# A list scheduler with other durations and a table of places, and block means spread by POOL

## The chip, the core and the metric

The kernel runs on one core of a Trainium2 chip. A core has TensorE (PE, with its weight loads listed as PEld), VectorE (DVE), ScalarE (ACT), GpSimd (POOL) and the queue of SyncE (SP), from which this kernel issues its DMAs. Each engine works through its own instructions in the order in which they were written and waits for the others by semaphores. The metric is the device time of one execution in microseconds, given as the median of several runs.

## What is computed

Four batches of 768 tokens with eight heads of 64. Each query sees its neighbours closer than 16 positions and, besides, 24 block keys and values, the maximum of 32 keys and the mean of 32 values. The attended rows pass through a mixer: one product pair over the tokens, with a residual, and one over the channels, with a residual. All is fp32.

```python
k_sum = k.reshape(B, H, nb, block, D).max(axis=3)
v_sum = v.reshape(B, H, nb, block, D).mean(axis=3)
...
a = np.exp(scores_all)
a = a / (np.sum(a, axis=-1, keepdims=True) + 1e-09)
v_all = np.concatenate([v, v_sum], axis=2)
return np.matmul(a, v_all).astype(np.float32)
...
h = np.maximum(xt @ w_tok1, 0.0) @ w_tok2
u = x + h.transpose(0, 2, 1)
h2 = np.maximum(u @ w_ch1, 0.0) @ w_ch2
return (u + h2).astype(np.float32)
```

## The kernel before

**What a batch does.** Heads are worked in pairs `p`, four to a batch. For each pair `scores` forms two groups `g` of score tiles in PSUM (L467). DVE masks each tile and takes its lowest value (`lowest`, L481), ACT takes the exponential and its sum (`power`, L491), twelve of each for a pair. In batches 0 and 1 `turn` transposes the result on PE (L529) and ACT evicts it (L540); in the later batches DVE and DMAs do so. `weighted` multiplies with the values (L599), POOL and DVE make the reciprocals (L605, L625), DVE scales (L610). `tok1` (L753) and `tok2` (L912, L920) are the two token products, `ch1` (L981) and `ch2` (L1024) the channel products, one slot for each of 24 blocks of the hidden layer. Each value is kept as a high and a low half, so a product is three matmuls. The last batch uses a scheme with fewer multiplications on sums of blocks of the weights; `mixes` makes these weight sums on POOL and ACT during the earlier batches and writes them to DRAM.

**The start.** There is no other batch to work on while the attention of batch 0 runs, which uses the PSUM banks `att`, `acc0` and `acc1`. Meanwhile the weights arrive as 64-bit words and are converted: `w_tick` `i` issues two DMAs (L1635), then an absolute value on ACT (L1665), a clamp on POOL (L1669), three integer operations on DVE (L1674, L1681, L1688), and, apart from the first three ticks, high halves on ACT (L1712) and low halves on POOL (L1718). Ticks 0 to 2 are the weight of `tok1`, 3 to 5 that of `tok2`, the rest the channel weights in the order in which `ch1` and `ch2` use them.

**Block keys and block means.** `key_blocks` takes the maxima of a pair's keys on DVE (L335) and copies them beside each window (L344). In batch 0 `first_means` makes the block means of a pair's values: 48 small matmuls (L361) leave two partial sums for each of the two heads in PSUM; ACT copies one of each to SBUF (L372). For the first head DVE adds the other (L382, `once`) and POOL spreads the result over the twelve tiles of the values (L387, `spread`). For the second head one DVE instruction adds and spreads at once (L375, `both`).

**What sets the order.** Nothing is issued directly. Every step is a `Work` handed to `Plan.add` with an engine, a duration ("hold") in microseconds, what it reads and writes, and a rank. `Plan._order` then plays the kernel: an engine that is free takes, of the works that are ready by the played clock, the one of least rank and, within a rank, of least number `seq`. The ranks are `R_H` 0, `R_EVAC` 1, `R_ATT` 2, `R_LATER` 3, `R_W` 4 and `R_MIX` 6. A work is ready when all that it needs has ended in the play, with an allowance `LATE` after another engine's work; a DMA takes its kilobytes by `RATE`, plus `LAND`. The order found so is written out and is the order of each engine's queue on the chip. The holds therefore do not change any instruction, but they decide which one stands ahead of which. `behind` holds a work back until another one has begun.

Of the kernel before, what the change touches and what calls it, by code (L numbers as in the profile page):

```python
# [15 lines left out]
ALU = mybir.AluOpType  # L16
# [55 lines left out]
class Work:  # L72
    def __init__(self, seq, eng, took, run, rank, kb):
        self.seq, self.eng, self.took, self.run, self.rank, self.kb = seq, eng, took, run, rank, kb
        self.takes, self.needs, self.behind = [], set(), set()
        self.start = self.end = None


class Plan:
    LATE = {"pe": 0.3, "act": 0.15, "dve": 0.15, "pool": 0.2, "sp": 0.0}  # L80
    RATE, LAND = 250.0, 2.2
# [46 lines left out]
    def _order(self):  # L128
# [9 lines left out]
        idle = {e: 0.0 for e in self.LATE}  # L138
        queues = {e: [] for e in self.LATE}
# [5 lines left out]
        for w in self.works:  # L145
            if not left[w]:
                release(w)
        while events:
# [51 lines left out]
def tile_attention_mixer(  # L200
# [89 lines left out]
    def load(slot, view, src, kb, reads=(), behind=()):  # L290
        return add(
            "sp", 0.06, lambda: nc.sync.dma_start(out=view(slot.t), in_=src),
# [13 lines left out]
    def load_v(n):  # L306
# [7 lines left out]
        state["v"] = load(slot, lambda t: t[:WIN], vw[b, h], 295)  # L314
        if b > 0:
            s = vs[b]
            add(
                "sp", 0.06,
# [9 lines left out]
    def key_blocks(p):  # L328

        if p >= B * NP:  # L330
# [3 lines left out]
            "dve", 0.98,  # L334
# [8 lines left out]
            "dve", 0.33,  # L343
# [7 lines left out]
    def first_means(p):  # L351
# [22 lines left out]
        def both(n):  # L374
            nc.vector.tensor_tensor(  # L375
                out=v_t[n].t[WIN:NC],
                in0=half(1, 1).unsqueeze(1).broadcast_to([NB, NT, D]),
                in1=s.t[WIN:NC, D:].unsqueeze(1).broadcast_to([NB, NT, D]), op=ALU.add,
            )

        def once():
            nc.vector.tensor_tensor(  # L382
                out=s.t[WIN:NC, :D], in0=half(0, 1), in1=s.t[WIN:NC, :D], op=ALU.add
            )

        def spread(n):
            nc.gpsimd.tensor_copy(  # L387
                v_t[n].t[WIN:NC], s.t[WIN:NC, :D].unsqueeze(1).broadcast_to([NB, NT, D])
# [3 lines left out]
            "pe", 0.9, sums, reads=[(v_t[2 * p], 0), (v_t[2 * p + 1], 0)], writes=[(pt, 0)],  # L392
# [1504 lines left out]
```

## Time and profile before

| | us |
|---|---|
| median of 3 runs | 560.07 |
| lowest and highest of them | 559.93, 560.61 |
| the profiled execution | 559.61 |
| its span, first to last instruction | 557.8 |

The profiled execution spends 1.81 us outside of its span. The rows that the prediction shows are of three kinds. Window rows give the busy time of each engine in a stretch, with the number of instructions. Timeline rows give start, duration, engine, line, operation, what it writes and reads, a count, and in brackets the idle time of the engine just before, with what ended it. Group rows give the sum and the mean of all instructions of one line and form.

### The profile page before, as it was taken

What the parts mean: (1) busy time and instruction counts of PE and PEld (TensorE: products, weight loads), DVE (VectorE), ACT (ScalarE), POOL (GpSimd) and SP (SyncE); (2) the same over time, 40 slices, a digit from 0 to 9 for tenths busy, and PEclk for the clock granted to TensorE, in tenths of its full rate; (3) what the DMA queues carried; (4) which work ended last, traced back from release to release, by engine and by line L of the source; (5) the groups of instructions that cost most, each with busy time, mean ns of one, the idle gap of its engine ahead of it and who ended that gap; (6) DMA issues with size and microseconds to landing.
All of it is one profiled execution on the core that took longest, in us unless ns stands there. A gap on an engine that the chain in (4) does not pass through costs nothing.

```text
span 557.8 us, 12595 instructions
## 1 busy us (share of the span) xinstructions
PE 544.0 (98%) x4557; PEld 479.6 (86%) x4557; DVE 330.3 (59%) x922; ACT 251.9 (45%) x784; POOL 246.8 (44%) x362
## 2 busy tenths in 40 slices
PE   7699999999999999999999999999999999999997
PEld 4588788888999978888799988878889999999997
DVE  4788999979365355454543247454352065669992
ACT  4786666625585344332323325343433453356410
POOL 0326687835574932310067404378769963000000
PEclk9999999999999999999999999999999999999999
DMA  8963668755668138768595316787696543932742
GB/s 277 330 189 108 215 209 249 240 163 190 203 187 251 42 131 226 198 207 226 146 253 137 104 29 196 160 237 198 171 259 168 135 155 116 333 95 81 219 134 85
DMA packets 125743, 101.10 MB, mean 181 GB/s; under 512 B 70000, under 2 KB 105456, under 8 KB 125680
## 3 DMA queue, kind: packets, MB, share of 16 engines
q1 hardware_dynamic: 125680, 100.29, 60.7%
q8 instruction: 36, 0.59, 0.5%
q14 instruction: 27, 0.22, 0.1%
HBM read 70.18 MB, written 28.31 MB: 177 GB/s over the span
## 4 chain that ended last, share of the span: by engine, by line
PE 90%; ACT 4%; DVE 3%; POOL 2%; issue 1%; ACTq 0%
PE acc L1024 27%; PE hp L981 27%; PE sc L467 4%; PE av L599 4%; PE up L920 3%; PE t1q L837 3%; ACT e L491 2%; PE x L1251 2%; PE y L1251 2%; PE z L1251 2%; PE pz L1251 2%; PE t1q L800 2%; PE up L1213 2%; PE warm L1731 1%; PE pw L1251 1%; PE pv L1251 1%
## 5 line engine op out<-in xcount | busy, mean ns | idle before, releaser
L1024 PE MATMUL acc<-h,w2h 128*128 128x256 f32 (+1 forms) x576 | 153.8, 339 | 0.0
L981 PE MATMUL hp<-u,w1h 128*128 128x256 f32 (+1 forms) x576 | 143.8, 339 | 0.0
L1024 PEld LDWEIGHTS acc<-h,w2h 128*128 128x128 f32 x576 | 100.6, 188 | 13.8 <-ACT h L993 1.6
L981 PEld LDWEIGHTS hp<-u,w1h 128*128 128x128 f32 x576 | 98.0, 189 | 12.4 <-issue 1.1
L981 PE MATMUL hp<-u,w1l 128*128 128x256 f32 (+1 forms) x288 | 96.9, 336 | 0.0
L491 ACT ACTIVATE e<-e,den 128x120 f32<-128x120 f32 x192 | 73.3, 384 | 52.0 <-DVE den L481 39.1
L1024 PE MATMUL acc<-h,w2l 128*128 128x256 f32 (+1 forms) x288 | 96.4, 335 | 0.0
L998 DVE SCALAR_TENSOR_TENSOR h<-hp,h 128x512 fp32r<-128x512 f32 (+1 forms) x72 | 39.9, 554 | 90.9 <-ACT h L993 90.7
L993 ACT ACTIVATE h<-hp 128x512 fp32r<-128x512 f32 (+1 forms) x72 | 35.2, 489 | 114.7 <-PE hp L981 114.5
L981 PEld LDWEIGHTS hp<-u,w1l 128*128 128x128 f32 x288 | 54.4, 189 | 5.8
L1024 PEld LDWEIGHTS acc<-h,w2l 128*128 128x128 f32 x288 | 54.2, 188 | 5.2
L481 DVE CUSTOM_DVE_ANT_0 e<-sc,mask_sb 128x120 f32<-128x120 f32 x192 | 41.7, 277 | 16.8 <-PE sc L467 16.2
L605 POOL TENSOR_SCALAR rec<-den 128x6 f32<-128x6 f32 x32 | 8.6, 269 | 66.1 <-ACT e L491 64.0
L491 ACT ACTIVATION_READ_ACCUMULATOR e<-e,den 128x1 f32 x192 | 36.1, 188 | 0.0
L1064 POOL TENSOR_TENSOR ot<-ot,u 128x512 f32<-128x512 f32 (+1 forms) x24 | 24.4, 1042 | 19.7 <-DVE ot L1056 18.2
L467 PE MATMUL sc<-k,q 64*64 64x120 f32 x768 | 28.0, 271 | 3.7 <-DVE den L481 2.2
L467 PEld LDWEIGHTS sc<-k,q 64*64 64x64 f32 x768 | 20.5, 132 | 12.5 <-issue 6.2
L920 PE MATMUL up<-wt2h,t 128*128 128x512 f32 (+1 forms) x96 | 28.4, 354 | 0.6 <-DVE t L739 0.6
L599 PEld LDWEIGHTS av<-v,eT 120*64 120x64 f32 x768 | 24.0, 138 | 4.7 <-issue 2.8
L599 PE MATMUL av<-v,eT 120*64 120x64 f32 x768 | 26.5, 224 | 0.9 <-PE hp L981 0.4
L335 DVE TENSOR_REDUCE ks<-k 128x24 f32<-128x768 f32 x16 | 15.2, 948 | 20.5 <-DMA k<-in_kw 20.5
L423 DVE TENSOR_REDUCE vs<-vb 96x8 f32<-96x256 f32 (+1 forms) x40 | 17.8, 458 | 9.4 <-DMA vb<-in_vb 9.3
(248 smaller groups left out, 1042.7 us busy)
## 6 DMA issues: line engine op xcount, KB each, us to landing
w<-in_w_ch SPq DMA_DIRECT2D x48, 256.0 KB
k<-in_kw SPq DMA_DIRECT2D x16, 720.0 KB
v<-in_vw SPq DMA_DIRECT2D x32, 288.0 KB
q<-in_q SPq DMA_DIRECT2D x16, 384.0 KB
away<-e SPq DMA_DIRECT2D x16, 384.0 KB
eT<-away SPq DMA_DIRECT2D x64, 96.0 KB
w<-in_w_tok SPq DMA_DIRECT2D x12, 256.0 KB
vb<-in_vb SPq DMA_DIRECT2D x32, 96.0 KB
```

Source lines behind the costliest of these rows:

```text
L423: lambda: nc.vector.tensor_reduce(out=s.t[:VB, rows], in_=slot.t[:VB], axis=AX, op=ALU.add),
L467: nc.tensor.matmul(tiles[j].t[c * QT : (c + 1) * QT, i * NC : (i + 1) * NC], lhsT=qt.t[rows, t * QT : (t + 1) * QT], rhs=kt.t[rows, t, :], ...
L481: nc.vector.tensor_tensor_reduce(out=e.t[:, j, i * P : i * P + NC], in0=tiles[j].t[:, i * NC : (i + 1) * NC], in1=mask_sb[:, mv, :], op0=A ...
L491: nc.scalar.activation(ei, ei, AF.Exp, bias=den_t[n].t[:, 1, T : T + 1], scale=-1.0, accum_out=den_t[n].t[:, 0, T : T + 1],)
L599: nc.tensor.matmul(pv[cs, T], lhsT=eT[:NC, T % (TT // 2), cs], rhs=v.t[:NC, 2 * T + c], start=True, stop=True,)
L920: nc.tensor.matmul(pt.t[:, :nt], lhsT=t1.t[:, part, ks], rhs=w.t[:, k, h0 : h0 + nt], start=(far and k == 0 and i == 0), stop=(k == DTOK / ...
L981: nc.tensor.matmul(pt.t[:, :nt], lhsT=block(w, f, c), rhs=us[c].t[:, part], start=(i == 0), stop=(i == len(ops) - 1),)
L993: lambda: nc.scalar.activation(h.t[:, 0], pt.t[:, :nt], AF.Relu),
L998: lambda: nc.vector.scalar_tensor_tensor(out=h.t[:, 1], in0=pt.t[:, :nt], scalar=0.0, in1=h.t[:, 0].bitcast(F32), op0=ALU.max, op1=ALU.sub ...
L1024: nc.tensor.matmul(slot.t[:, c0 : c0 + nt], lhsT=block(w, f, o), rhs=h.t[:, part], start=(f == 0 and w == "w2h" and part == 0 and o % n == 0),
L1064: lambda view=view, u=u: nc.gpsimd.tensor_tensor(out=view(), in0=view(), in1=u.t[:, 1].bitcast(F32), op=ALU.add),
L1251: nc.tensor.matmul(pt.t[:, :cols], lhsT=w[wp][0](), rhs=z.t[:, zp], start=first and seen == 0, stop=final and seen == 3 * len(ops) - 1, sk ...
```

## The change

It has five parts.

1. The play in `Plan` gets other constants: first times for each engine (`FIRST`), a time after the hold in which the result becomes visible (`DRAIN`), a time in which the waiting engine notices (`NOTICE`), and a DMA that takes `BEGIN`, kilobytes by 375, and `LAND`.
2. Nearly every hold is replaced. A DMA issue on SP is 0.44 instead of 0.06, and the kilobytes of value loads and of weight loads are given as 413 and 375 instead of 295 and 262.
3. `Work.place` takes the part of (rank, seq) in the play's queues, and the table `PLACES` gives 45 works of the start, by number, another place.
4. In `first_means` the second head is treated as the first: `once` on DVE, `spread` on POOL; `both` is gone.
5. `TOKT` goes from 3 to 7, so ticks 3 to 6 get rank 2 instead of 4; and the weight sum `('w2', 4, 'h')` is handed in at slot 21 of batch 2 instead of slot 14, held behind the `ch1` of that slot.

The numbers in `PLACES` count the works of the changed kernel. Read in the code, they are: the second pair's first value load ahead of the first pair's second (9); the queries of pair 3 (128); thirteen of `lowest`, ten of pairs 1 and 3 to the front (108, 114, 116, 118, 237 to 247) and three of pairs 0 and 2 to behind later works (20, 22, 140); exponentials (23, 56, 60, 145, 273); evictions (51, 182, 184, 316); `once` and `spread` (123, 125, 217, 219, 284, 286) and a partial sum (216); scalings, reciprocals and low halves on DVE (97, 188, 192, 197, 255); steps of ticks 2 to 6 (88, 153, 163, 173, 227); the copy of block keys (147); on PE one `tok1` (261), one transpose (289), and the second score group of pair 3, which goes from rank 0 to rank 4 (267).

```diff
+        self.place = (rank, seq)
...
+PLACES = {
+    9: (0, 7.1), 20: (2, 61.7), 22: (2, 63.4), 23: (1, 128.8), 51: (1, 128.9), 56: (1, 128.2),
+    60: (1, 128.7), 88: (2, 14.2), 97: (2, 190.5), 108: (2, 13.9), 114: (2, 16.1),
+    116: (2, 62.6), 118: (2, 16.3), 123: (2, 16.2), 125: (2, 63.2), 128: (0, 7.7),
+    140: (2, 206.8), 145: (4, 305.5), 147: (2, 206.1), 153: (2, 206.2), 163: (2, 206.4),
+    173: (2, 78.1), 182: (2, 247.5), 184: (2, 247), 188: (2, 190.7), 192: (2, 15.6),
+    197: (2, 278.5), 216: (4, 392.4), 217: (2, 205.4), 219: (2, 14.8), 227: (4, 505.6),
+    237: (2, 15.5), 239: (2, 13.8), 241: (2, 15.3), 243: (2, 190), 245: (2, 14.3),
+    247: (2, 14.8), 255: (2, 204.8), 261: (2, 197.9), 267: (4, 618.7), 273: (4, 506.5),
+    284: (2, 79.8), 286: (2, 79.2), 289: (2, 198.6), 316: (4, 391.6),
+}
...
-    LATE = {"pe": 0.3, "act": 0.15, "dve": 0.15, "pool": 0.2, "sp": 0.0}
-    RATE, LAND = 250.0, 2.2
+    FIRST = {"pe": 1.17, "act": 1.9, "dve": 0.85, "pool": 1.2, "sp": 0.7}
+    DRAIN = {"pe": 0.16, "act": 0.1, "dve": 0.08, "pool": 0.045, "sp": 0.0}
+    NOTICE = {"pe": 0.035, "act": 0.035, "dve": 0.035, "pool": 0.09, "sp": 0.035}
+    SEEN, BEGIN, LAND, RATE = 0.06, 1.34, 1.0, 375.0
...
+        w.place = PLACES.get(w.seq, w.place)
...
-                    heapq.heappush(queues[w.eng], (w.rank, w.seq, w))
+                    heapq.heappush(queues[w.eng], (w.place, w.seq, w))
...
-                    dma = max(dma, now) + w.kb / self.RATE
+                    dma = max(dma, now + self.BEGIN) + w.kb / self.RATE
                     w.end = dma + self.LAND
                 else:
-                    w.end = now + w.took
+                    w.end = now + w.took + self.DRAIN[e]
...
-                    late = self.LATE[e] if n.eng != e else 0.0
-                    at = w.end + late if whole else now
+                    if not whole:
+                        at = now + self.SEEN
+                    elif n.eng != e:
+                        at = w.end + self.NOTICE[n.eng]
+                    else:
+                        at = idle[e] if e == "pe" else w.end
...
-        def both(n):
+        def once(j):
+            cs = slice(j * D, (j + 1) * D)
             nc.vector.tensor_tensor(
-                out=v_t[n].t[WIN:NC],
-                in0=half(1, 1).unsqueeze(1).broadcast_to([NB, NT, D]),
-                in1=s.t[WIN:NC, D:].unsqueeze(1).broadcast_to([NB, NT, D]), op=ALU.add,
-            )
...
+                out=s.t[WIN:NC, cs], in0=half(j, 1), in1=s.t[WIN:NC, cs], op=ALU.add
+            )
...
+        for j in range(2):
+            add(
+                "dve", 0.2, lambda j=j: once(j), reads=[(pt, 0)], writes=[(s, j)], rank=R_EVAC
+            )
+            add(
+                "pool", 0.95, lambda j=j: spread(j), reads=[(s, j)],
+                writes=[(v_t[2 * p + j], 1)], rank=R_ATT,
+            )
...
-                    "act", 0.39, lambda n=n, j=j, i=i: power(n, j, i), reads=[(den, ("min", T))],
+                    "act", 0.379, lambda n=n, j=j, i=i: power(n, j, i), reads=[(den, ("min", T))],
...
-            "pe", 12 * nt / 2220, products,
+            "pe", 12 * nt / 2170, products,
...
-    TOKT = 3
+    TOKT = 7
...
-    add("pe", 7.0, warm_up, reads=[(warm, 0)], writes=[(pw, 0)])
+    add("pe", 4.6, warm_up, reads=[(warm, 0)], writes=[(pw, 0)])
...
-(2, 14): [('w2', 4, 'h')]
+(2, 21): [('w2', 4, 'h')]
...
-                mixes(*job)
+                mixes(*job, behind=here if slot > 14 else ())
```

More of the change, by code (lines that the diff above doesn't have):

```diff
@@ L137, in _order @@
         ready = {w: 0.0 for w in self.works}
-        idle = {e: 0.0 for e in self.LATE}
-        queues = {e: [] for e in self.LATE}
+        idle = dict(self.FIRST)
+        queues = {e: [] for e in idle}
         events, done, dma = [], [], 0.0
@@ L147, in _order @@
                 release(w)
+        for e, at in idle.items():
+            heapq.heappush(events, (at, -1, None))
         while events:
@@ L291, in load @@
         return add(
-            "sp", 0.06, lambda: nc.sync.dma_start(out=view(slot.t), in_=src),
+            "sp", 0.44, lambda: nc.sync.dma_start(out=view(slot.t), in_=src),
             reads=reads, writes=[(slot, 0)], kb=kb, behind=[*behind, *state["gate"]],
@@ L534, in turn @@
             add(
-                "pe", 0.5, flip, reads=[(e, (j, i)) for i in range(TT // 2)], writes=[(pt, 0)],
+                "pe", 0.33, flip, reads=[(e, (j, i)) for i in range(TT // 2)], writes=[(pt, 0)],
                 rank=R_H,
@@ L620, in weighted @@
             add(
-                "pool", 0.15, whole, reads=[(den, ("sum", T)) for T in range(TT)],
+                "pool", 0.166, whole, reads=[(den, ("sum", T)) for T in range(TT)],
                 writes=[(rec, 0)], rank=R_H,
@@ L759, in tok1 @@
         add(
-            "pe", 2.8, products, reads=x_keys(b, p) + [(wt1, i) for i in range(3)],
+            "pe", 2.68, products, reads=x_keys(b, p) + [(wt1, i) for i in range(3)],
             writes=[(pt, 0)], rank=R_ATT,
@@ L808, in tok1x @@
             add(
-                "pe", 1.45, products, reads=[(s, i) for s in parts for i in range(2)],
+                "pe", 1.44, products, reads=[(s, i) for s in parts for i in range(2)],
                 writes=[(pt, 0)], rank=R_ATT,
@@ L843, in tok1_all @@
             add(
-                "pe", 1.37, products, reads=[(s, i) for s in (xs, ws) for i in range(2)],
+                "pe", 1.376, products, reads=[(s, i) for s in (xs, ws) for i in range(2)],
                 writes=[(pt, 0) for pt in pts], rank=R_ATT,
@@ L1039, in ch2 @@
             add(
-                "pe", 12 * nt / 2220, lambda: products(range(NC4)), reads=reads,
+                "pe", 12 * nt / 2170, lambda: products(range(NC4)), reads=reads,
                 writes=[(slot, 0) for slot in slots], rank=R_W,
@@ L1079, in tile_attention_mixer, with mixes @@
     mix_t, sum_t, plain = {}, {}, {}
[L1081 removed]
+    def mixes(k, i, tag, half=None, behind=()):
         n = 256 if half is None else P
@@ L1098, in mixes @@
             add(
-                "pool", n * 0.0043 + 0.19, lambda x=x, f=f: whole(x, f),
-                reads=weight_keys(names, f), writes=[(a, x)], rank=R_MIX,
+                "pool", n * 0.0043 + 0.145, lambda x=x, f=f: whole(x, f),
+                reads=weight_keys(names, f), writes=[(a, x)], rank=R_MIX, behind=behind,
             )
@@ L1219, in tok2_last @@
         add(
-            "pe", 1.08, products, reads=t1_keys(b, p) + T2_KEYS, writes=[(pt, 0)], rank=R_ATT
+            "pe", 1.05, products, reads=t1_keys(b, p) + T2_KEYS, writes=[(pt, 0)], rank=R_ATT
         )
         add(
-            "dve", 0.56,
+            "dve", 0.474,
             lambda: nc.vector.tensor_tensor(
@@ L1259, in product @@
         return add(
-            "pe", 3 * len(ops) * cols / 2190, run, reads=list(reads), writes=[(pt, 0)], rank=R_W
+            "pe", 3 * len(ops) * cols / 2215, run, reads=list(reads), writes=[(pt, 0)], rank=R_W
         )
@@ L1637, in w_tick @@
                 ),
-                writes=[keys[j]], kb=262, behind=behind,
+                writes=[keys[j]], kb=375, behind=behind,
             )
@@ L1736, in tile_attention_mixer @@
     add(
-        "sp", 0.06, lambda: nc.sync.dma_start(out=mask_sb, in_=mask), writes=[("mask", 0)], kb=184
+        "sp", 0.44, lambda: nc.sync.dma_start(out=mask_sb, in_=mask), writes=[("mask", 0)], kb=184
     )
```

152 lines of the change are left out of this document (70 added, 82 removed).

## The prediction

> **What bounds the kernel now.** I read the page first, for the share of each engine and for the chain that ended last.
>
> ```profile
> span 557.8 us, 12595 instructions
> PE 544.0 (98%) x4557; PEld 479.6 (86%) x4557; DVE 330.3 (59%) x922; ACT 251.9 (45%) x784; POOL 246.8 (44%) x362
> PE 90%; ACT 4%; DVE 3%; POOL 2%; issue 1%; ACTq 0%
> ```
>
> PE is busy nearly throughout, and nine tenths of the chain are PE. The change removes no matmul, so what can be won is PE's idle time. Where that lies the window view tells (start and end, length, then busy time and instructions of PE, PEld, DVE, ACT and POOL, granted clock, DMA share, GB/s):
>
> ```profile
> 8.00:64.00 56.00, 47.32 (x780) 39.97 (x769) 46.81 (x167) 42.35 (x156) 23.55 (x35) 1.00 0.72 220
> 64.00:558.00 494.00, 489.87 (x3746) 436.64 (x3744) 281.59 (x751) 208.30 (x628) 222.50 (x321) 1.00 0.60 175
> ...
> 8.00:20.00 12.00, 8.61 (x230) 6.53 (x222) 8.98 (x53) 10.57 (x50) 1.30 (x3) 1.00 1.04 326
> 20.00:32.00 12.00, 7.85 (x119) 6.25 (x109) 10.49 (x36) 7.35 (x25) 4.18 (x6) 1.00 1.00 295
> 32.00:44.00 12.00, 12.00 (x288) 10.93 (x284) 10.59 (x43) 10.75 (x41) 5.14 (x9) 1.00 0.52 149
> ...
> 467.00:558.00 91.00, 87.27 (x502) 86.93 (x500) 65.64 (x103) 34.92 (x63) 2.93 (x4) 1.00 0.50 159
> ```
>
> From 8 to 64 us PE idles 56.00 - 47.32 = 8.68 us. From 64 us to the end it idles 494.00 - 489.87 = 4.13 us, and 91.00 - 87.27 = 3.73 us of that is the last stretch, whose end is the drain behind the last matmul. So 0.4 us are left to win in 490 us, and 8.7 us in the first 64. Nearly all of it lies before 32 us (3.39 + 4.15 us). There DVE and ACT take turns as the limit: ACT 10.57 of 12 us, then DVE 10.49 of 12. The granted clock is 1.00 in all these rows. PE's timeline shows what ends the idle times:
>
> ```profile
> 11.91 1.09 PE L467 MATMUL sc<-k,q 64*64 64x120 f32 x24 [0.55 <-DVE den L481]
> 12.92 1.13 PE L361 MATMUL vm<-v,means 96*24 96x64 f32 x48
> 13.98 0.87 PE L529 MATMUL et<-identf,e 128*120 128x128 f32 x6
> 16.16 1.22 PE L467 MATMUL sc<-k,q 64*64 64x120 f32 x24 [1.30 <-ACT eT L540]
> 22.77 1.04 PE L467 MATMUL sc<-k,q 64*64 64x120 f32 x24 [1.63 <-DVE den L481]
> 27.71 0.71 PE L753 MATMUL t1p<-x,wt 128*128 128x128 f32 x4 [0.98 <-DVE wt L1688]
> 29.71 2.05 PE L753 MATMUL t1p<-x,wt 128*128 128x128 f32 x16 [1.28 <-DVE wt L1688]
> ```
>
> These five waits make 5.74 of the 8.68 us. Since PE is full behind them, a microsecond saved here is one saved at the end, as long as the weights keep up (below).
>
> **The change part by part.**
>
> *Block means.* DVE's queue around the third of these waits, and the groups concerned:
>
> ```profile
> 20.88 0.22 DVE L382 TENSOR_TENSOR vs<-vm,vs 24x64 f32<-24x64 f32 x1 [0.72 <-ACT vs L372]
> 21.13 0.96 DVE L375 TENSOR_TENSOR v<-vm,vs 24x768 f32<-24x768 f32 x1
> 22.11 0.31 DVE L344 COPY k<-ks 128x288 f32<-128x288 f32 x1
> ...
> L375 DVE TENSOR_TENSOR v<-vm,vs 24x768 f32<-24x768 f32 x4 | 3.9, 965 | 0.1
> L387 POOL COPY v<-vs 24x768 f32<-24x768 f32 x4 | 3.3, 824 | 6.3 <-DVE vs L382 6.0
> ...
> 31.69 1.62 PE L599 MATMUL av<-v,eT 120*64 120x64 f32 x48
> ```
>
> Each pair trades a DVE instruction of 0.965 us for one of 0.22 (L382), so DVE gains 0.74 us four times, 2.98 in all, and POOL takes four more copies of 0.82 us. In pair 1 the long instruction stands right ahead of the key copy and of the `lowest` for which PE waits until 22.77: **-0.74**. In pair 0 DVE waits for PE afterwards. In pairs 2 and 3 (32 to 46 us) PE is full and ACT almost, 10.75 of 12. There the gain is between 0 and 3 x 0.74 = 2.23; I take **-0.4**, near the lower end, because ACT sets the pace. The second head's values come 0.82 us later, behind the first head's copy; the product of the first head lies between (48 of these matmuls take 1.62 us for both heads, by half 0.81), so this costs nothing, and up to 0.8 us where that cover fails.
>
> *POOL beside DVE.* The same instruction alone and beside POOL:
>
> ```profile
> 38.74 0.69 DVE L1681 SCALAR_TENSOR_TENSOR wb<-w,wb 128x512 int32<-128x512 int32 x1
> 54.70 1.11 DVE L1681 SCALAR_TENSOR_TENSOR wb<-w,wb 128x512 int32<-128x512 int32 x1
> 54.27 2.14 POOL L1718 TENSOR_TENSOR w1l<-wb,w1h 128x256 fp32r<-128x256 f32 x2 [1.80 <-ACT w1h L1712]
> ```
>
> DVE's conversion takes 0.42 us more where it meets POOL. Four more copies may cost DVE 0 to 4 x 0.42 = 1.7 us; many of its instructions there are `lowest`, which read PSUM, so I take **+0.2**. The Trainium skill (SBUF — State Buffer, section "SBUF: two separate sides") says that DVE, when it reads two operands from SBUF, and POOL share a pair of ports that one of them holds for its whole instruction while the other is blocked. By that rule each copy could cost a DVE conversion its full 0.82 us, 3.3 in all, and the sum below would be about +0.3 instead of -2.8. The pair of rows at 54 us agrees with it.
>
> *Places and holds in the start.* They reorder the queues of DVE, ACT and PE, and SP's by two loads. Two neighbours of `lowest` and two of the exponentials give their pace, 0.20 and 0.38 us:
>
> ```profile
> 8.49 0.28 DVE L481 CUSTOM_DVE_ANT_0 e<-sc,mask_sb 128x120 f32<-128x120 f32 x1
> 8.69 0.28 DVE L481 CUSTOM_DVE_ANT_0 e<-sc,mask_sb 128x120 f32<-128x120 f32 x1
> ...
> 9.00 0.38 ACT L491 ACTIVATE e<-e,den 128x120 f32<-128x120 f32 x1
> 9.38 0.38 ACT L491 ACTIVATE e<-e,den 128x120 f32<-128x120 f32 x1
> ```
>
> The first wait (0.55) is for work behind a row of `lowest`; the table puts two of these behind the key maxima, 2 x 0.20: **-0.4**. The waits for the first weights (0.98 + 1.28 = 2.26) are between 0 and 2.26 to be had. The old play let DMAs run at 250 GB/s while the rows above show 326 and 295, so the loads of keys, values and weights came in the play later than in truth, and PE's queue was cut to that. The new one is nearer; I take half, **-1.1**. Of the 1.30 us for the eviction I take a third, **-0.4**, since exponentials and evictions move on ACT, with 0 and 1.30 as ends. Loading pair 1's first values ahead of pair 0's second delays the latter by one load, 288 KB at 326 GB/s or 0.9 us (an estimate), and so the sums at 12.92 and the transposes queued on PE behind them at 13.98. The wait of 1.30 us before 16.16 covers this; without it, +0.9. Part of this queue is guessed: which order the play writes I can't read off the diff.
>
> *Ticks 3 to 6 earlier.* They compete on ACT with exponentials of pairs 2 and 3. Cover: `tok2` products that become ready sooner fill PE. I cost it at 0; the other end is a rival.
>
> *Later stages.* All holds change, by a few per cent where the rows are, and PE waits 0.4 us there. I take 0, with 0.4 to gain and about 1 us to lose (an estimate: some waits like the one of 0.61 us at 60.71, for an operand of `tok2`). That wait, the moved weight sum and the `ch1` that holds it:
>
> ```profile
> 60.71 0.73 PE L920 MATMUL up<-wt2h,t 128*128 128x512 f32 x2 [0.61 <-DVE t L739]
> 445.31 0.41 PE L981 MATMUL hp<-u,w1h 128*128 128x256 f32 x2
> 448.49 2.54 POOL L1095 TENSOR_TENSOR wa_w_None<-w2h,w2l 128x512 f32<-128x512 f32 x2 [2.35 <-DMA mix_w2h<-wa_w_None]
> ```
>
> The `ch1` behind which it is now held starts at 445.31 (slot 21, the tenth of this half), and the sum itself starts at 448.49, since it waits for the buffers of the sum before. The new hold ends earlier than that wait, so it costs and saves nothing; one POOL instruction of 1.27 us ahead of others is the bound both ways.
>
> Sum, in the order of the parts: -0.74 - 0.4 + 0.2 - 0.4 - 1.1 - 0.4 = -2.84. The span becomes 555.0 us and the profiled execution, which has 1.81 us around it, 559.61 - 2.84 = 556.8. The median lies 0.46 us above that execution, so I forecast **557.2 us**.
>
> **The rivals.**
>
> *More of the idle time goes.* All five waits vanish: -5.74 + 0.2 = -5.5, or **554.6 us**. For it: POOL is busy for 1.30 + 4.18 + 5.14 = 10.6 of the 36 us before 44, so there is room for four copies. Against it: the first exponentials need 12 x 0.38 us on ACT whatever the order.
>
> *The weights become the bound.* Low halves on POOL, and the chain's rows of the channel products that need them:
>
> ```profile
> 69.42 1.46 POOL L1718 TENSOR_TENSOR w1l<-wb,w1h 128x256 fp32r<-128x256 f32 x2 [0.59 <-ACT w1h L1712]
> 64.19 5.46 PE hp L981 x24
> 72.37 2.72 PE hp L981 x12
> ...
> 80.00:127.00 47.00, 47.00 (x229) 38.63 (x228) 42.34 (x75) 22.16 (x55) 29.74 (x44) 1.00 0.67 213
> ```
>
> The third block is ready at 70.9 and used at 72.4: 1.5 us of slack, and DVE is busy for 42.34 of 47 us. If PE arrives 2.8 us sooner and the conversions don't, PE waits 1.3 us there and again at later blocks, until only the first term is left: -0.74, **559.3 us**. Against it: DVE's own 2.98 us come ahead of these conversions.
>
> *DVE and POOL block each other.* Half of the bound by rows and more: -2.84 + 1.5 = -1.3, **558.7 us**. It decides if the copies meet conversions and not `lowest`.
>
> *Slower: conversions ahead of exponentials.* Before, ticks 3 to 6 had these pieces on ACT behind the last exponentials of pair 3:
>
> ```profile
> 46.23 0.39 ACT L491 ACTIVATE e<-e,den 128x120 f32<-128x120 f32 x1
> ...
> 47.92 0.42 ACT L1712 ACTIVATE wt2h<-wb 128x256 fp32r<-128x256 f32 x1
> 48.98 0.73 ACT L1712 ACTIVATE wt2h<-wb 128x256 fp32r<-128x256 f32 x2 [0.64 <-DVE wb L1688]
> 49.61 0.65 ACT L1665 ACTIVATE wb<-w 128x512 f32<-128x512 f32 x1
> ```
>
> With rank 2 and lower numbers they go first: four high halves at 0.42 and one absolute value at 0.65, 2.3 us by which the last exponentials come later. If the `tok2` products are not ready in that gap, PE waits it out. With only the first term on the other side: 2.3 - 0.74 = +1.5, **561.6 us**. It decides when PE waits over 0.7 us for L491 between 40 and 50 us.
>
> *Little changes.* If the play writes nearly the old order, only the block means count: this is the case of 559.3 again.
>
> **How the numbers follow.** Forecast 0.45, more of it 0.21, weights or little change 0.13, ports 0.06, slower 0.15. A measurement of this kernel tells about 0.2% from no change, 1.1 us: faster is below 558.95, slower above 561.2. The forecast and the larger gain are faster, the ports by half, the weights same: faster 0.69, same 0.16, slower 0.15. The range goes from 553.9, the larger gain with 0.4 from the later stages and a little of pairs 2 and 3, to the slower case, 561.6; beyond its ends I leave 0.07 and 0.10.
>
> **What would show it.** In the window view PE's idle time from 8 to 64 us falls from 8.68 to 5 or 6, DVE's busy time there by 3 us, and POOL gets eight instructions at L387. The wait of 1.63 us for `lowest` goes to under 1, those for L1688 halve. The first channel product starts near 61 us instead of 64.2. From 64 us on PE's idle time stays at 4. I would be wrong if PE waits for L1718 or L1688 between 64 and 100 us, for exponentials between 40 and 50, or if new idle time stands in the later batches.

## The result and the profile after

The median is 589.66 us (588.43 to 590.43, 5 runs) against 560.39 us for the kernel before on the same chip: a ratio of 1.0515, 95% interval 1.0494 to 1.0536. The kernel is 5% slower, and the forecast was 0.5% faster. The profiled execution took 588.43 us. From its page, the span, the first line of the engines and the chain that ended last:

```profile
span 586.6 us, 12627 instructions
PE 552.5 (94%) x4557; PEld 485.2 (83%) x4557; DVE 321.9 (55%) x922; ACT 253.2 (43%) x784; POOL 249.1 (42%) x366
PE 64%; DMA 14%; DVE 8%; SPq 5%; issue 4%; POOL 3%; ACT 2%; DVEq 0%; POOLq 0%; ACTq 0%
```

The matmuls are the same 4557. PE was 90% of the chain, now it is 64%, and DMAs with SP's queue hold 19%. The window view (columns as in the prediction) tells where the 28.8 us of span went:

```profile
8.00:64.00 56.00, 47.63 (x793) 41.48 (x793) 45.57 (x168) 43.04 (x156) 27.28 (x39) 0.97 0.73 216
64.00:587.00 523.00, 498.01 (x3747) 441.21 (x3745) 274.44 (x750) 208.84 (x627) 221.11 (x321) 0.99 0.57 166
8.00:20.00 12.00, 9.15 (x223) 7.35 (x224) 6.94 (x47) 9.60 (x45) 2.06 (x4) 0.86 1.03 329
20.00:32.00 12.00, 8.29 (x159) 6.80 (x155) 10.81 (x41) 9.12 (x33) 4.67 (x7) 1.00 1.03 293
```

In the start PE idles 8.37 us (before: 8.68), and the first channel product begins at 64.08 us (before: 64.02). Between these two executions nothing was won there and nothing lost. Behind 64 us PE idles 523.00 - 498.01 = 24.99 us (before: 4.13), 20.9 more, and for the same matmuls it is busy 498.01 - 489.87 = 8.1 us longer. Both together are the 29 us. Who ends PE's idle time behind 64 us, in the view of waits (total, times, longest; two more rows, of 0.5 and 0.2 us, are left out):

```profile
PE av L616 <- DMA eT<-away: 11.0, 4, 4.1
PE av L616 <- issue: 5.1, 3, 2.1
PE sc L484 <- DMA q<-in_q: 2.3, 1, 2.3
PE t1q L854 <- POOL xs L898: 1.3, 1, 1.3
PE av L616 <- DMA v<-vs: 0.6, 1, 0.6
```

The kernel before has one wait in that view behind 64 us, 0.4 us long, and none of these; three of the five rows name a DMA. One of them in PE's timeline, the value products of pair 12:

```profile
371.65 0.57 PE L616 MATMUL av<-v,eT 120*64 120x64 f32 x12
374.82 0.91 PE L616 MATMUL av<-v,eT 120*64 120x64 f32 x12 [2.60 <-DMA eT<-away]
375.67 0.80 PE L1041 MATMUL acc<-h,w2h 128*128 128x512 f32 x1
376.26 0.63 PE L1041 MATMUL acc<-h,w2l 128*128 128x512 f32 x1
376.69 1.05 PE L1041 MATMUL acc<-h,w2h 128*128 128x512 f32 x2
...
378.63 0.61 PE L1041 MATMUL acc<-h,w2h 128*128 128x512 f32 x2
```

PE takes its queue in order. It came to `av` at 371.65 and stood there for 2.60 us; the channel products behind it then ran without a wait of their own. SP's queue, same kernel, shows why `eT` was not there:

```profile
363.20 0.33 SPq L573 DMA_DIRECT2D away<-e  x1
...
365.36 0.63 SPq L591 DMA_DIRECT2D eT<-away  x1
...
371.11 1.36 SPq L591 DMA_DIRECT2D eT<-away  x2
```

From the second `away` (363.20) to the last fetch (the second of the two at 371.11, at 371.82) the chip took 8.62 us. In the scheduler's own clock, as its list gives it, the same two issues stand at 338.61 and 343.89, 5.28 us apart. The list, which is the order that the scheduler writes together with the start and end that it played for each work, had these issues 3.3 us closer together than they were, and PE paid most of that. The transfer itself was hardly longer than played: the last fetch landed 2.87 us after its issue by the trace, and the list has 2.74. Here SP's issues were late.

The stall has a second price. Behind it two matmuls of `acc` take 1.05 us, a moment later 0.61. The windows around it (next to last columns: granted clock, DMA share):

```profile
371.10:374.51 3.41, 1.12 (x18) 0.84 (x16) 1.02 (x2) 1.69 (x4) 2.56 (x6) 1.00 0.89 178
374.51:377.93 3.42, 3.11 (x17) 2.58 (x18) 0.56 (x1) 0.00 (x0) 1.22 (x2) 0.50 0.42 138
377.93:381.34 3.41, 3.41 (x39) 2.77 (x38) 0.71 (x2) 0.00 (x0) 0.14 (x1) 1.00 0.52 141
```

A stretch of 3.41 us in which PE idles for 2.29 us is followed by one at half clock. The trace's clock records have four of these behind 64 us (from 121.93, 309.66, 374.51 and 449.61), and none in the profiled execution of the kernel before. Four times 3.41 us at half speed, with a full PE, are 6.8 of the 8.1 us by which PE is busy longer. How much of that reaches the end is not shown: the run n2 below has 20.5 us of half clock behind 64 instead of 13.7, and its time from there on is the same.

### The profile page after: what moved, and what is told of

It is laid out like the page before. It is cut to its first block, busy times and chain, and to the rows that moved or that the text cites. A ratio compares the mean times of both kernels' runs of the same rounds, so it can differ in the third digit from the quotient of the medians.

```text
span 586.6 us, 12627 instructions
## 1 busy us (share of the span) xinstructions
PE 552.5 (94%) x4557; PEld 485.2 (83%) x4557; DVE 321.9 (55%) x922; ACT 253.2 (43%) x784; POOL 249.1 (42%) x366
## 3 DMA queue, kind: packets, MB, share of 16 engines
q1 hardware_dynamic: 125680, 100.29, 58.4%
## 4 chain that ended last, share of the span: by engine, by line
PE 64%; DMA 14%; DVE 8%; SPq 5%; issue 4%; POOL 3%; ACT 2%; DVEq 0%; POOLq 0%; ACTq 0%
PE acc L1041 16%; PE hp L998 14%; SPq L591 4%; PE sc L484 3%; PE t1q L854 3%; PE av L616 3%; DMA away<-e 3%; PE up L937 3%; DMA k<-in_kw 2%; PE x L1268 2%; PE y L1268 2%; PE pz L1268 2%; PE z L1268 2%; DMA w<-in_w_ch 2%; DMA vb<-in_vb 2%
## 5 line engine op out<-in xcount | busy, mean ns | idle before, releaser
L1041 PE MATMUL acc<-h,w2h 128*128 128x256 f32 (+1 forms) x576 | 158.3, 347 | 0.0
L1041 PEld LDWEIGHTS acc<-h,w2h 128*128 128x128 f32 x576 | 103.7, 194 | 14.5 <-ACT h L1010 1.6
L1041 PE MATMUL acc<-h,w2l 128*128 128x256 f32 (+1 forms) x288 | 98.5, 342 | 0.0
L1041 PEld LDWEIGHTS acc<-h,w2l 128*128 128x128 f32 x288 | 55.9, 194 | 5.3
L616 PE MATMUL av<-v,eT 120*64 120x64 f32 x768 | 28.6, 228 | 18.8 <-DMA eT<-away 11.0
L616 PEld LDWEIGHTS av<-v,eT 120*64 120x64 f32 x768 | 25.2, 139 | 23.9 <-issue 17.7
```

The costliest lines, as they stand in the source:

```text
L616: nc.tensor.matmul(pv[cs, T], lhsT=eT[:NC, T % (TT // 2), cs], rhs=v.t[:NC, 2 * T + c], start=True, stop=True,)
L1041: nc.tensor.matmul(slot.t[:, c0 : c0 + nt], lhsT=block(w, f, o), rhs=h.t[:, part], start=(f == 0 and w == "w2h" and part == 0 and o % n == 0),
```

## The experiments

**Theory A**: the scheduler's new figures for DMAs are too short, so works that DMAs feed stand too early in PE's queue. **Rivals**: B, the new holds and the smaller allowances between engines; C, the table of places with the earlier ticks; the moved weight sum. All runs together; "first" is the start of the first channel product, "rest" the time from there to the last matmul, both from the profiled execution. "Late" is the share of DMAs issued behind 64 us that landed later than the scheduler's list had it: by the trace from the issue to the last update of the DMA's semaphore, against the same interval in the list. That and the half clock are worked out from the traces.

| run | median us | ratio to before, 95% interval | first | rest | late | half clock behind 64 |
|---|---|---|---|---|---|---|
| before | 560.39 | | 64.02 | 490.25 | 14% | 0 |
| after | 589.66 | 1.0515 (1.0494-1.0536) | 64.08 | 519.03 | 46% | 13.7 |
| e1_old_dma | 570.59 | 1.0171 (1.0131-1.0211) | 70.86 | 494.58 | 9% | 0 |
| e2_new_dma | 579.29 | 1.0324 (1.0288-1.0361) | 64.39 | 510.40 | 45% | 6.8 |
| d1_rate_land | 583.30 | 1.0394 (1.0348-1.0439) | 68.00 | 508.37 | 40% | 0 |
| f4_fetch_margin | 587.92 | 1.0472 (1.0421-1.0523) | 63.52 | 519.92 | 39% | 17.1 |
| f5_all_margin | 562.81 | 1.0032 (1.0016-1.0049) | 63.55 | 493.71 | 5% | 0 |
| g1_rate_later | 561.76 | 1.0017 (1.0001-1.0034) | 63.43 | 493.34 | 5% | 3.4 |
| g3_allowances | 567.38 | 1.0135 (1.0110-1.0160) | 64.22 | 497.90 | 8% | 6.8 |
| e4_no_places | 596.33 | 1.0638 (1.0588-1.0688) | 73.68 | 517.67 | | |
| e4b_table_out | 589.82 | 1.0535 (1.0486-1.0585) | 66.17 | 519.44 | | |
| e3_means | 567.14 | 1.0109 (1.0082-1.0137) | 71.89 | 490.51 | | |
| f1_means_same_order | 563.00 | 1.0038 (1.0024-1.0053) | 67.32 | 490.25 | | |
| h1_copies_behind | 562.75 | 1.0049 (1.0028-1.0070) | 66.58 | 489.50 | | |
| e5_sum_moved | 560.18 | 0.9998 (0.9978-1.0017) | 63.52 | 490.92 | | |
| e6_ticks_early | 563.32 | 1.0053 (1.0031-1.0075) | 67.86 | 489.50 | | |
| s1_start_of_after | 558.54 | 0.9952 (0.9935-0.9970) | 64.12 | 489.16 | | 0 |
| n1_splice_fill | 558.73 | 0.9969 (0.9953-0.9985) | 64.41 | 488.65 | | 0 |
| n2_after_fill | 587.44 | 1.0466 (1.0414-1.0518) | 64.85 | 518.98 | | 20.5 |

The medians belong to several sittings, in which the kernel before lay between 560.1 and 561.2; the ratios are each to its own. "First" and "rest" come from one execution each. Five lists that begin alike (after, f4, f5, g1, g3) have their first channel product between 63.43 and 64.22 us, so differences under a microsecond there tell nothing.

### The figures for DMAs

**Old figures in the kernel after, new figures in the kernel before.** The core of the first edit; the second makes the reverse one in the kernel before. All of SP's holds and the KB go with them:

```diff
-    SEEN, BEGIN, LAND, RATE = 0.06, 1.34, 1.0, 375.0
+    SEEN, BEGIN, LAND, RATE = 0.06, 1.34, 2.2, 250.0
...
-                    dma = max(dma, now + self.BEGIN) + w.kb / self.RATE
+                    dma = max(dma, now) + w.kb / self.RATE
...
-            "sp", 0.44, lambda: nc.sync.dma_start(out=view(slot.t), in_=src),
+            "sp", 0.06, lambda: nc.sync.dma_start(out=view(slot.t), in_=src),
```

> The kernel after, but with the old figures for DMAs in the scheduler: each issue holds SP 0.06 us (0.4 for the round trips), 250 GB/s, 2.2 us to land, the old KB. All holds of PE, DVE, ACT and POOL, the table of places, the block means and the moved weight sum stay new. Theory A (new DMA figures are too short, so works that DMAs feed stand too early in PE's queue): the waits of PE after 64 us fall from 25.0 to under 8 us, the median to 557 to 566 us. Theory B (new compute holds and the smaller allowances between engines do it): 580 to 592 us, the waits at av L616 stay. Theory C (table of places and earlier ticks): 580 to 592 us too.

> The kernel before, with only the new figures for DMAs in the scheduler: each issue holds SP 0.44 us, a transfer begins 1.34 us after its issue, 375 GB/s, 1.0 us to land, the new KB. Theory A: PE waits for eT<-away and for keys, queries and values return in the later batches, 572 to 592 us. Theory B and theory C: 556 to 563 us, PE idle after 64 us stays under 6 us.

With the old figures the rest falls from 519.0 to 494.6 us; with the new ones alone it rises from 490.3 to 510.4. Theory A holds from both sides, for 20 to 24 of the 28.8 us. The median of e1, 570.59 us, is above the 557 to 566 that A gave, since its start is 6.8 us longer. What the new holds and allowances cost behind the start, theory B, is at most the 4.3 us that e1 keeps against before, as long as the old figures for DMAs stand beside them.

**The transfer alone, in the kernel before** (no change of SP's hold and of the KB):

```diff
-    RATE, LAND = 250.0, 2.2
+    RATE, LAND = 375.0, 1.0
...
-                    dma = max(dma, now) + w.kb / self.RATE
+                    dma = max(dma, now + 1.34) + w.kb / self.RATE
```

> The kernel before, with of the new DMA figures only the transfer (begins 1.34 us after its issue, 375 GB/s, 1.0 us to land); SP's hold of an issue and the KB stay old. With all of the new DMA figures the time from the first channel product to the end was 510.4 us against 490.3. If the shorter transfers are what does it: 503 to 512 us here too. If the longer hold of SP does it: 490 to 494 us.

508.4 us: of the 20 us, 18 come with begin, rate and landing, and SP's hold and the KB have little to do with it. Begin and landing together are 2.34 us against 2.2 before, so the rate is the part of it that differs.

**Only the round trip of `eT` gets a margin.**

```diff
                     w.end = dma + self.LAND
+                    if w.kb == 150:
+                        w.end += 3
```

> The kernel after; in the scheduler alone each of the 64 fetches of eT is taken to land 3.0 us later. The order is that of after up to 215 us of its clock; the scheduler's own end stays at 551.3 us. Theory A (PE's queue holds av too early for the round trip of eT, and nothing else of the later batches matters as much): PE's waits at av L616 for eT<-away, 11.0 us, and most of the 5.1 us put to issue go, PE behind them is not slowed; 588-590 falls to 566 to 574 us; about 8 us of loss from before 215 us stays. Theory B (holds and allowances of the engines): 584 to 592 us, the waits go elsewhere.

A clean miss for theory A: 587.92 us lies in the range written down for theory B, and the next two runs have to decide. PE's waits behind 64 us in this run:

```profile
PE av L618 <- issue: 5.1, 3, 2.7
PE t1q L856 <- POOL xs L900: 4.0, 2, 2.0
PE sc L486 <- DMA q<-in_q: 2.0, 1, 2.0
PE t1q L856 <- ACT xs L892: 2.0, 2, 1.8
PE up L931 <- DVE x L629: 2.0, 1, 2.0
PE av L618 <- DMA eT<-away: 1.4, 2, 0.8
```

The wait named most in the profile after, 11.0 us for `eT`, is down to 1.4, and behind the start nothing is won (519.92 against 519.03 us): other waits take its place. 39% of the DMAs are still late.

**Every DMA gets a margin, or only the rate is the old one, behind 60 us.**

First f5, then g1:

```diff
                     w.end = dma + self.LAND
+                    if now > 60.0:
+                        w.end += 3.0 if w.kb == 150 else 2.0
```

```diff
-                    dma = max(dma, now + self.BEGIN) + w.kb / self.RATE
+                    rate = self.RATE if now < 60.0 else 250.0
+                    dma = max(dma, now + self.BEGIN) + w.kb / rate
```

> The kernel after; in the scheduler alone every DMA issued behind 60 us is taken to land 2.0 us later, the fetches of eT 3.0. The start stays that of after (first channel product near 64.1 us). Theory A: the time from the first channel product to the end falls from 519.0 to 490 to 497 us, median 559 to 567; the waits of PE for keys, queries and values at 118 us go too. Theory B: 575 to 590 us.

> The kernel after; in the scheduler every DMA issued behind 60 us moves at 250 GB/s as before, and not at 375; begin, landing, SP's hold and KB stay new, and a single transfer of 96 KB ends only 0.2 us later. With 2 to 3 us more for every landing the time from the first channel product to the end was 493.7 us, in after 519.0. If the rate (how transfers queue behind each other) makes most of the loss: 490 to 502 us. If the landing does: 508 to 520 us.

Both give what theory A asks. All the waits that PE has left behind 64 us, first with the margins, then with the rate:

```profile
PE acc L1043 <- DVE ot L1075: 0.8, 1, 0.8
PE sc L486 <- PE et L548: 0.7, 1, 0.7
PE z L1270 <- ACT sums_t L1287: 0.6, 1, 0.6
PE acc L1043 <- DVE h L1017: 0.5, 1, 0.5
PE up L931 <- DVE den L500: 0.3, 1, 0.3
PE w L1270 <- DMA w1h<-mix_w1h: 0.2, 1, 0.2
```

```profile
PE up L930 <- DVE den L499: 2.5, 1, 2.5
PE z L1269 <- ACT sums_t L1286: 0.2, 1, 0.2
```

So one number, 375 in the place of 250, makes 25.7 of the 28.8 us, although it moves the end of a lone `eT` fetch, 150 KB in the list, by 0.2 us only. In the list the transfers stand behind one another at this rate; at 250 the DMAs behind 64 us land 1.61 us before the list expects them (median), at 375 they land 0.05 us before it. The new figures were therefore right on average: nearly half of the DMAs came late, 16% of all by over 1 us, and a late one that feeds PE holds everything behind it. The old ones were wrong by over a microsecond, on the side that costs little while PE has other work to put ahead: f5, whose margins are 2 to 3 us, keeps 3.5 us against before. The rate acts as such a margin, and it covers late issues too: g1 has no wait for `eT` left, with SP's hold still at 0.44.

**The allowances between engines.** g1 leaves 3.1 us behind 64, and the one wait of 2.5 us for `lowest` in its view stands for most of them. This run takes g1 and lets every result reach another engine 0.15 us later:

```diff
                         at = w.end + self.NOTICE[n.eng]
+                        if now > 60.0 and not w.kb:
+                            at += 0.15
```

> The kernel after; in the scheduler behind 60 us 250 GB/s, and 0.15 us more from the end of a work to its use on another engine. With the rate alone the time from the first channel product to the end was 493.3 us, in before 490.3, with one wait of 2.5 us for lowest at 205 us. If the smaller allowances between engines are the rest: 489 to 491.5 us, no wait over 1 us behind 64, median 557.5 to 560. If not: 493 to 497 us.

It is worse, 497.9, with new waits of 2.4 us (`hp` for ACT) and 1.3 us (`t1q` for POOL). Which figure put that work too early in g1 stays open; theory B isn't shown by it.

### The start

**The block means alone.** Once with the scheduler free to write a new list (e3), once with every engine's list kept as before (f1):

```diff
         def both(n):
             nc.vector.tensor_tensor(
-                out=v_t[n].t[WIN:NC],
-                in0=half(1, 1).unsqueeze(1).broadcast_to([NB, NT, D]),
-                in1=s.t[WIN:NC, D:].unsqueeze(1).broadcast_to([NB, NT, D]), op=ALU.add,
+                out=s.t[WIN:NC, D:], in0=half(1, 1), in1=s.t[WIN:NC, D:], op=ALU.add
             )
+            nc.gpsimd.tensor_copy(
+                v_t[n].t[WIN:NC], s.t[WIN:NC, D:].unsqueeze(1).broadcast_to([NB, NT, D])
+            )
```

> The kernel before, with the block means alone changed: both heads added at 24x64 and spread by POOL, holds and scheduler old. By the prediction's terms -0.74 for pair 1, -0.4 for pairs 2 and 3, +0.2 for POOL beside DVE: 0.9 us less, 559.4 us by the median of before, and the wait of 1.63 us for lowest at 22.77 goes under 1. If PE's order or the next wait takes it back: 560 to 561 us. If the scheduler's order shifts in the later stages as well: more than 562 us, with new idle time after 64 us.

> The kernel before with the block means of after, but each engine keeps the order of before: the second head's addition at 24x64 stands where the addition at 24x768 stood on DVE, its copy on POOL right behind. The run with the block means alone lost 7.9 us before the first channel product (71.89 against 64.02 us) and 0.3 after. Theory D (the scheduler, given other works, wrote a worse order of the start; the instructions themselves cost nothing or gain a little, as the prediction's terms have it): first channel product at 63 to 64.3 us, median 559 to 561. Theory E (POOL's copies themselves are late, or block DVE): first channel product at 66 to 72 us, median 562 to 568.

With a new list 7.9 us are lost before the first channel product, and none behind it, which is none of the three outcomes written down. With the old list 3.3 are lost in the profiled execution and 2.1 by the ratio (0.38%). By the written ranges f1 falls to theory E. So the larger part is the list, and the instructions don't come free either. POOL and DVE in f1:

```profile
22.31 0.97 POOL L378 COPY v<-vs 24x768 f32<-24x768 f32 x1 [3.54 <-DVE vs L375]
23.22 0.82 POOL L388 COPY v<-vs 24x768 f32<-24x768 f32 x1
24.13 0.61 POOL L1670 TENSOR_SCALAR wt<-wt 128x512 f32<-128x512 f32 x1
```

```profile
24.78 0.43 DVE L1675 TENSOR_SCALAR wt<-wt 128x512 int32<-128x512 int32 x1 [1.69 <-POOL wt L1670]
```

DVE is free earlier, as forecast, and then waits 1.69 us for the clamp of the first weights, which stands on POOL behind the new copy. The next run puts POOL's second copies of pairs 1 to 3 behind these clamps, by moving three entries of the list.

> The run with the block means of after in the order of before (first channel product 67.32 us, median 0.4% above before), with one difference: POOL's second copies of pairs 1, 2 and 3 stand behind the next conversions of weights on POOL (pair 1 behind three of them), since their products come later. Theory F (the copies stood ahead of the clamps L1670 that the first weights wait for): DVE's wait of 1.69 us for L1670 at 24.78 goes, first channel product at 63 to 65 us, median 558.5 to 561. Theory G (POOL beside DVE, or anything else of the copies): first channel product still at 66 to 67.5 us, median 562 to 564.

The wait for L1670 falls to 0.44, and the time hardly changes, as theory G has it. So the clamps' place isn't the whole of it. By the traces the clamp's own input, the absolute value on ACT, ends at 22.31 in before, at 23.36 in f1 and at 23.65 in h1; POOL's queue adds 0.6 us to that in f1 and nothing in h1. Pair 1's sums on PE are late already (20.38 and 20.50 against 19.47). Two things, which no run took away, name what else is there. The first is the clock. In PE's timeline of f1 and then of h1 stands `tok1`; in the kernel before these sixteen products start at 29.71 and take 2.05 us:

```profile
31.38 3.78 PE L754 MATMUL t1p<-x,wt 128*128 128x128 f32 x16 [1.28 <-DVE wt L1689]
```

```profile
31.49 3.65 PE L902 MATMUL t1p<-x,wt 128*128 128x128 f32 x16 [1.71 <-DVE wt L1837]
```

Of the 3.3 us that f1 loses in this execution, 1.67 are there when they start, and 1.73 come while they run. The granted clock is 0.50 there, from 30.03 to 36.86 us in f1 and from 31.46 to 34.87 in h1. Each has one more such stretch ahead of pair 1's sums or beside them, from 12.96 and from 17.81 us; the profiled execution of before has none in its start. The second is DVE beside POOL's copies in h1:

```profile
22.52 0.82 POOL L536 COPY v<-vs 24x768 f32<-24x768 f32 x1 [4.82 <-DVE vs L531]
28.53 1.16 POOL L536 COPY v<-vs 24x768 f32<-24x768 f32 x1
```

```profile
22.75 0.76 DVE L499 COPY k<-ks 128x288 f32<-128x288 f32 x1
29.14 0.84 DVE L1823 TENSOR_SCALAR wt<-wt 128x512 int32<-128x512 int32 x1
```

The key copy takes 0.31 us in before and the conversion 0.42, so DVE loses 0.45 and 0.42 us to these two meetings. In f1 the key copy starts ahead of the POOL copy, at 22.28, and keeps its 0.31; there it is the POOL copy that takes 0.97 instead of 0.82.

**Earlier ticks, the moved sum, the table.** Ticks alone (`TOKT = 7` in the kernel before) and the sum alone (slot 21 and its hold); then the kernel after without the table, the ticks and the sum (e4), and without the table only (e4b).

```diff
-    TOKT = 3
+    TOKT = 7
```

```diff
-(2, 14): [('w2', 4, 'h')]
+(2, 21): [('w2', 4, 'h')]
...
-                mixes(*job)
+                mixes(*job, behind=here if slot > 14 else ())
```

```diff
-        w.place = PLACES.get(w.seq, w.place)
...
-                    heapq.heappush(queues[w.eng], (w.place, w.seq, w))
+                    heapq.heappush(queues[w.eng], (w.rank, w.seq, w))
```

> The kernel before with one change: weight ticks 3 to 6 get the rank of attention work. The prediction's step: 0, so first channel product near 64.0 us; its slower rival: conversions go ahead of exponentials of pair 3, 2.3 us, first channel product at 66 to 67 us. From there to the end 490 to 491 us both ways.

> The kernel before with one change: the last weight sum begins at slot 21 instead of 14 and is held behind the product of that slot. The prediction's step: 0, within one POOL instruction of 1.27 us both ways. First channel product at 64 us, from there to the end 489.5 to 491.5 us. If the moved sum costs part of the loss: over 492 us, with PE waiting for mixed weights behind 440 us.

> The kernel after without the table of places, with ticks 3 to 6 at their old rank and the weight sum at its old slot: new scheduler, new holds, new block means alone. Theory A and theory B: the loss stays, 578 to 595 us, with PE waits at av L616 for DMAs in the later batches. Theory C (the table, the earlier ticks or the moved sum cause the loss): 555 to 562 us.

> The kernel after without the table of places alone (earlier ticks and moved sum kept). Without all three the first channel product came at 73.68 us, in after at 64.08. If the table makes the start: 72 to 77 us here. If the earlier ticks do, under the new scheduler: 64 to 67 us. From there to the end 515 to 521 us both ways.

Under the old scheduler the ticks lose 2.9 us (0.53%). Under the new one the ticks with the sum win 73.68 - 66.17 = 7.5 us of the start, and the table 66.17 - 64.08 = 2.1 more, each from one execution; the ratios give 1.0% and 0.2%, and the 0.2% lie within the intervals. Neither touches the rest: theory C is out, although e4's median, 596.33, is 1.3 us above what A and B gave. The sum alone costs nothing.

**Is it the half clock?** The start of after has one stretch at half clock, from 12.70 us, behind a wait of 2.53 us. In the last two runs PE gets matmuls of the warm-up kind to do in such waits, 18 in four places on top of the run s1 below, or 7 in one place of the kernel after:

```diff
+    def fill(n):
+        for _ in range(n):
+            nc.tensor.matmul(pw.t, lhsT=warm.t[:, :P], rhs=warm.t, start=True, stop=True)
```

> The run with the start of after and the later order of before (558.5 us), with 18 matmuls of the warm-up kind (128x512, their result is not used) put into PE's queue ahead of four works that wait in the start: 7 ahead of the scores of pair 1 behind the wait of 2.53 us, 3 ahead of the next scores, 4 ahead of a transpose and 4 ahead of a value product. Theory H (a stretch of 3.41 us in which PE idles by over 2 us is followed by 3.41 us at half clock, and two of these, from 13.18 and 26.83 us, cost that run 3.4 us): no half clock between 10 and 60 us, first channel product at 60.5 to 62 us, median 555 to 557. Theory I (the clock isn't set by PE's idle time, or the start is bound by DVE and ACT): first channel product at 63.5 to 64.5 us, median 558 to 560; later if the fillers are in the way.

> The kernel after with the 7 matmuls of the warm-up kind ahead of the scores of pair 1, and nothing else. Theory H: the half clock from 12.70 to 16.11 us goes, first channel product at 62 to 63 us; the four half clocks behind 64 us and the waits ahead of them stay, from the first channel product to the end 517 to 521 us. Theory I: first channel product at 64 us.

n1 had no half clock at all before its end, s1 had 6.8 us of it in the start, and the first channel product comes at 64.41 against 64.12. The clock part of theory H holds, its price doesn't in this start: PE waits for DVE and ACT anyway, and a slow PE uses up idle time. The fillers take time of PE as well (the value product that s1 starts at 25.47 starts at 26.63 in n1), so n1 doesn't price the clock by itself. n1's windows:

```profile
8.00:20.00 12.00, 9.43 (x220) 6.34 (x220) 6.63 (x44) 9.49 (x44) 2.07 (x4) 1.00 1.03 337
20.00:32.00 12.00, 10.79 (x179) 7.77 (x177) 10.81 (x43) 9.05 (x33) 4.70 (x7) 1.00 0.93 259
```

DVE's 10.81 us of 12 are those of after, to the hundredth. n2 moved the half clock from 12.70 to 19.49 us and won nothing either; its first channel product is 0.8 us later.

The other executions of the kernel before belong here too. Of the 78 that lie below 564 us in these sittings, nine have a mean granted clock of 1.000, as the profiled one has, and take 558.6 to 559.5 us. Most, 49, have 0.994, which is two stretches of 3.41 us at half clock, and their median is 1.2 to 1.8 us higher within each sitting that has both kinds. So in the kernel before the half clock goes with a longer time; no trace of these executions was kept, and where the stretches lie isn't known.

### A version that beats both

s1 has the kernel of after (with the sum at its old slot), but the list is fixed: the 360 works that after's scheduler starts before 58.4 us of its clock, and behind them the rest in the order of before.

```diff
-        for w in self._order():
+        for w in (self.works[i] for i in ORDER):
```

> Block means of after; each engine's order is that of after up to 58 us of its scheduler's clock (360 works), and behind it that of before. Theory A (the start of after is as good as that of before, all of the loss is the order behind it): first channel product at 63.5 to 64.3 us, from there to the end 489.5 to 492 us, median 558.5 to 562. If works that the new start leaves behind are missed later: over 564 us.

It takes 558.54 us, and the kernel before 560.40 in the same sitting; the ratio is 0.9952 (0.9935 to 0.9970), so 0.3 to 0.65% are won. Its row behind 64 us:

```profile
64.00:557.00 493.00, 488.98 (x3747) 435.79 (x3745) 282.31 (x750) 208.23 (x628) 222.49 (x321) 1.00 0.60 176
```

PE idles 4.02 us there, 4.13 before and 24.99 in after: with the old list behind the new start the whole loss is gone. That shows that all of it is the order behind the start, and none of it the instructions. Where s1's gain arises isn't shown: its profiled execution has 64.12 and 489.16 us against 64.02 and 490.25 in before.

## Why the prediction was wrong

**The bound** was read rightly: PE, with 8.7 us to win in the start and 0.4 behind it. The conclusion was not. "No change behind 64 us" needs PE's queue to stay as good there, and the change rewrote that queue from end to end.

**Later stages: the step that failed.** "I take 0, with 0.4 to gain and about 1 us to lose" stood against +28.8 us: the term was put at nothing although the change gives every queue behind 64 us a new order. The bound of 1 us came from a wait of before, 0.61 us at 60.71, which lies in the start. But a nearly full queue shows how good the old list is, not how much another list can lose. How much, g1 tells: one figure of the scheduler, the rate, holds 25.7 us.

**"The new one is nearer"** was the argument on the DMA figures in the part on the places, from 326 and 295 GB/s in two windows against 250. It is true (median error behind 64 us 0.05 us, against 1.12 in before) and it points the wrong way. A list that an in-order queue follows loses when a transfer is late and gains little when it is early (f5); a figure that is right on average is late about half of the time, here 46%. The page had this to see: 326 and 295 GB/s come from windows whose DMA share is 1.00 or more, and both are under the 375 that the diff takes.

**Block means**: -0.74, -0.4 and +0.2 were forecast, about +2 measured in the old order. DVE's shorter instruction is there (0.23 us in f1 against 0.96). The step that failed is "the product of the first head lies between, so this costs nothing": it looked at who waits for the copies and not at what stands behind them on POOL, the clamps of the first weights. Part of the +2 may be the half clock that f1 and h1 show in their starts. POOL beside DVE was put at +0.2; two meetings in h1 cost 0.87 us. The rule of the Trainium skill (SBUF — State Buffer, section "SBUF: two separate sides") that was weighed there agrees with these rows in kind: of two instructions that meet, the one that started second took longer. No run tested it by itself.

**Ticks 3 to 6**: 0 was forecast, with a rival of 2.3 us. Alone under the old scheduler they cost 2.9: the rival had the size. Its place was wrong; PE waits for POOL there, not for exponentials:

```profile
PE av L599 <- POOL wt2l L1718: 2.3, 1, 2.3
```

Under the new scheduler the same edit wins.

**Places**: of the forecast waits, those for the first weights (2.26 us) and of 1.63 us for `lowest` are gone from after. A new one of 2.53 us for `lowest` ahead of pair 1's scores took their place. The sum for the start was -2.84; the first channel product shows +0.06, and between -0.6 and +0.2 in f4, f5, g1 and g3, whose lists begin alike. By the medians s1, which has this start, is 1.9 us faster than before. That this lies near 2.84 is no proof of the terms: the block means and the ticks, each alone in the old scheduler's order or list, lose 2 to 3 us, and the prediction itself says that it could not read off the order.

**The moved sum**: 0 forecast, 0.9998 (0.9978 to 1.0017) measured.

**The rivals**: none of the five held the outcome. The slower one was a single mechanism in the start, while the part of the change that reaches over the whole kernel had no rival of its own. What the prediction named as a sign against itself, "new idle time in the later batches", is what came.

## What to carry to other kernels

A scheduler's durations are bounds, not measurements: where the consumer's queue runs in order, take a transfer's time near its late end, because in these runs early cost little while other work could go ahead, and late stopped all that stood behind. When a change retimes a scheduler, look at the stages that are already full first; they have next to nothing to win, and the loss isn't bounded by the waits that they show now. And test a list's figures against the trace one DMA at a time: the share that lands later than the list says (14% before, 46% after, 5% in f5 and g1) told good lists from bad, where the largest wait in the profile pointed at one kind of transfer whose margin alone was worth nothing.

## What the runs showed of the hardware

**The clock.** Every record of a half clock between the start and the last matmul lasts 3.41 us or a multiple in these traces. In the kernel after, the stretches of 3.41 us ahead of them had PE idle for 2.3 to 2.5 us; stretches with up to 1.8 us idle weren't followed by one. The profiled execution of the kernel before has at most 1.6 us in any, and no half clock until its end. The border isn't sharp: in s1 a stretch with 1.77 us idle (from 23.42) was followed by one, in e4 one with 1.17 (from 23.85), while one with 1.90 in e1 (from 7.37) wasn't. The Trainium skill (TensorE: Matmul & The Clock Gate, section "What's actually happening") says that the clock falls to one half after an idle window of about 3.4 us. The length agrees with the records here, but the window didn't have to be idle throughout: a third of it was enough in e4, and about two thirds in after.

**What an issue holds.** Eight `eT` fetches of pair 12 occupied SP's queue 0.56 to 1.60 us each, 0.66 in the middle, where the list holds SP for 0.44; the 32 loads of values in the same trace occupied it 0.40 us in the middle:

```profile
L591 SPq DMA_DIRECT2D eT<-away x8: 557/658/1598, 365.4 to 371.8; - x8
```

**How wide landings spread.** From issue to the last semaphore update, the 64 fetches of `eT` in after took 2.5 to 6.6 us (median 3.1), the 32 loads of values 2.9 to 10.1 (median 4.3), by the trace. The list had 2.9 and 4.0 us in the middle.
